# Reordering ScalarE's squares and GpSimd's sums inside the slots of a fused Fourier filter and SwiGLU kernel

## The chip, the cores and the metric

The kernel runs on one core of a Trainium2 chip. A core has five engines that each work through their own queue of instructions in order: TensorE (PE in the profile, its weight loads PEld), VectorE (DVE), ScalarE (ACT), GpSimd (POOL) and SyncE (SP), which here only issues transfers. Sixteen DMA engines move data between the chip's memory and the core, and also transpose tiles inside the core. Matmul results land in eight banks of accumulator memory (PSUM), 512 single-precision numbers wide per partition; an engine must have read a bank before TensorE may write it again.

The metric is the device time of one execution in microseconds (us). Every time below is in us unless it says otherwise.

## What is computed

```python
# x: 8 x 3008 x 256; 1505 frequencies; d_ff = 1536
X = np.fft.rfft(x, axis=1)
Y = X * (filt_r + 1j * filt_i)[None]
y = np.fft.irfft(Y, n=3008, axis=1).reshape(24064, 256)
rms = np.sqrt(np.mean(y * y, axis=-1, keepdims=True) + 1e-06)
yn = y / rms * rms_g
g, v = yn @ w_gate, yn @ w_val
out = (g * (1.0 / (1.0 + np.exp(-g))) * v) @ w_out
```

All inputs and the output are single precision. The kernel multiplies in half precision and accumulates in single precision.

## The kernel before

**The Fourier part** is done for one of the 8 batches `b` at a time, as matmuls with constant tables, because 3008 = 47 x 64:

- *Stage A* (`a_unit`, 12 units a batch): one matmul of 512 columns (`psa`), evicted to `t`; every three units are stored to memory (`z_store`) and loaded back in another layout (`t2_load`).
- *Stage B* (`b_unit`, 16 units): four small matmuls (`psb`, in bank `mb`). VectorE multiplies the result with two parts of the filter (`s_part`, lines 233 and 236), and GpSimd adds the two products into `ss` (`add_unit`, line 270: the "sum"). After two units a transposing transfer on SyncE's queue makes `yt` from `ss` (`yt_load`).
- *The inverse of stage B* (`bi_unit`, 16 units): four small matmuls on `yt` (`psi`, bank `mx`), evicted by ScalarE into `uu` (line 197). All of `uu` is transposed by four transfers (`t4_load`).
- *The inverse of stage A with the norm*, in 6 blocks `m` of up to 512 rows: `n_unit` makes two column blocks of 256 with one matmul (`psn`, bank `mx`) and evicts them to `y`; `sq_unit` squares them on ScalarE, two instructions `junk` (line 324) with a row sum each; `stat_unit` makes the reciprocal root on GpSimd (`u` and `rho`, lines 332 and 334: the "root"); `xt_unit` multiplies `y` with it on GpSimd (`xt`, line 342: the "row scale"); `tr_unit` transposes `xt` into `xn` with a transfer on SyncE's queue.

A few units take other forms: batch 0 and its first blocks go another way before the main loop, and `b_soft` moves both products of four stage B units of batch 1 to GpSimd.

**The feed-forward part** is the main loop. Its items are (batch, block, `jt`) with `jt` from 0 to 11 over the 1536 hidden columns in steps of 128: 576 items. One pass of the loop is a *slot*, numbered like its item; in it `gv` issues two matmuls for the gate (`pg`) and two for the value (`pv`), each over the block's 512 rows (384 in the last block of an even batch), then ScalarE's `sg` and VectorE's `hh`; then come the planned units of that slot; last `down` issues four matmuls (`po`; three for 384 rows) that use the `hh` of two slots before. `pg` and `pv` have two banks each, so four banks serve `gv`; two serve `po`, and `mx` and `mb` the Fourier units. Stage A uses `mx`, or `mb` where that suits better.

**The plan** is a dictionary from a slot to a list of units, filled ahead of the loop: while the loop works on batch `b-1`, the Fourier part of batch `b` is spread over its slots. `fit` looks for a slot in which bank `mx` (`"M"`) or `mb` (`"B"`) is free and the estimated load of ScalarE and VectorE stays within bounds. Units of one slot are issued in list order, and each engine's queue has that order. `at` appends a unit to its slot's list, except those in `front`, which it puts at the head. A batch's second product is planned in the slot after its stage B unit, the sum one slot later, and `yt_load` one slot after every second sum; `sq_unit` stands in the slot after its `n_unit`. `stat_unit`, `xt_unit` and `tr_unit` stand 2, 3 and 7 slots after the second `n_unit` of their block from batch 2 on.

```python
front = (sq_unit, s_part)
...
        if fn in front:
            todo.insert(0, (fn, a))
        else:
            todo.append((fn, a))
...
                    s0 = fit(slots[i], *need)
                    at(s0, b_unit, b, i, 0 if k == "M" else 3)
                    at(s0 + 1, s_part, b, i, 1)
                    at(s0 + 2, add_unit, b, i)
```

Of the kernel before, what the change touches and what calls it, by code (L numbers as in the profile page):

```python
# [100 lines left out]
def kernel(  # L101
# [510 lines left out]
    with tc.manual_schedule():  # L612
# [76 lines left out]

        items = [(b, m, jt) for b in range(B) for m in range(6) for jt in range(JT)]  # L690
        plan, late = {}, {}
        front = (sq_unit, s_part)
        load = {r: [0.0] * (len(items) + 99) for r in "MBAV"}
        room = {"A": 0.8, "V": 0.7}
        for i in range(JT + 1, len(items), JT):
# [29 lines left out]
        def norm_plan(b, m, slots, r):  # L725
            for i in range(2):
                s = fit(slots[i], ("M", 0, 1), ("A", 0, 0.6), ("A", 1, 0.82))
                at(s, n_unit, b, m, i)
                at(s + 1, sq_unit, b, m, i)
            for d, fn in zip(r, (stat_unit, xt_unit, tr_unit)):  # L730
                at(s + d, fn, b, m)
            assert s + r[-1] + 1 < 72 * b + 12 * m
# [49 lines left out]
        for b in range(1, B):  # L782
# [18 lines left out]
            for m in range(6):  # L801
                norm_plan(b, m, (n_at + 8 * m, n_at + 8 * m + (4 if b > 1 else 2)), (2, 3, 7) if b > 1 else (2, 3, 6))

        stores = {}
        for i in range(len(items) + 4):
            if i < len(items):
# [46 lines left out]
```

## Time and profile before

| | us |
|---|---|
| median of 3 runs | 873.1 |
| lowest, highest | 871.36, 873.5 |
| the profiled execution, whole | 872.03 |
| its span, first to last instruction | 870.3 |
| mean granted TensorE clock in it | 0.998 of full |

The page gives for every engine the time that it was busy, its share of the span and the number of its instructions. The chain of work is followed back from the last instruction to what released each step; its shares say whose work set the end. A wait is shown with the engine that waited, its line, and what ended it. In rows in order of time the first number is the start from the beginning of the span, the second the length; then follow engine, line, operation, output and inputs, shape, count, and in brackets an idle time before it with what ended it. A row of the view of stretches gives a stretch's bounds and length, then for each engine the busy time with the number of instructions in it, then the granted clock, the share of the DMA engines and the rate in GB/s. A matmul's end is modelled in these records, its start is not.

### The profile page before, as it was taken

The page shows a single profiled execution, that of the slowest core. Times are in us where ns is not written, and L with a number is a line of the kernel's source. Part 1 is how long each engine was busy: PE and PEld are TensorE (multiplying, and loading weights), DVE is VectorE, ACT ScalarE, POOL GpSimd, SP SyncE. Part 2 cuts the span into 40 slices and gives each one's busy share as a digit, 9 for nine tenths or more (in the row PEclk, how much of TensorE's full clock was granted, in tenths as well). Part 3 has the DMA queues.
Part 4 walks back from the last instruction along what each step waited for, and adds up shares of the span by engine and source line. Part 5 has one row for each costly group of instructions (what it writes and reads, how often), then busy time and mean ns, then how long its engine had stood idle before and what let it go on. Part 6 is the DMA issues. An engine that isn't in the chain of part 4 may idle for free.

```text
span 870.3 us, 17008 instructions
## 1 busy us (share of the span) xinstructions
PE 852.1 (98%) x6129; PEld 533.0 (61%) x6129; DVE 559.9 (64%) x936; ACT 612.1 (70%) x1352; POOL 295.5 (34%) x340
## 2 busy tenths in 40 slices
PE   6999999999999999999999999999999999999997
PEld 5755666566665566666566666666666666665664
DVE  5856765776666666666576666667666766555554
ACT  4787777787577766877578765788567865777443
POOL 4813841454143421444034430443214440132000
PEclk9999999999999999999999999999999999999999
DMA  9986678655976666744656666634474331522101
GB/s 283 270 149 156 119 152 191 147 117 139 188 146 124 126 134 131 146 110 101 143 120 136 125 124 136 148 87 92 122 142 92 72 91 43 109 67 49 62 25 49
DMA packets 198605, 107.98 MB, mean 124 GB/s; under 512 B 158966, under 2 KB 182904, under 8 KB 198520
## 3 DMA queue, kind: packets, MB, share of 16 engines
q1 hardware_dynamic: 189896, 85.52, 44.4%
q0 software_dynamic: 8480, 21.24, 12.2%
q8 instruction: 48, 0.79, 0.4%
q14 instruction: 37, 0.30, 0.1%
q10 hardware_dynamic: 144, 0.13, 0.0%
HBM read 45.78 MB, written 35.65 MB: 94 GB/s over the span
## 4 chain that ended last, share of the span: by engine, by line
PE 93%; DVE 2%; DMA 2%; ACT 2%; issue 1%; POOL 0%; POOLq 0%; ACTq 0%
PE po L565 27%; PE pg L548 27%; PE pv L548 26%; PE psb L243 3%; PE psi L287 2%; PE psn L316 2%; PE psa L208 2%; DMA xc<-in_x_dram 1%; PE psy L419 1%; DVE hh L553 1%; DMA yt<-ss 1%; ACT sg L552 1%; PE psf L390 1%; ACT uu L197 0%; PE pst L369 0%
## 5 line engine op out<-in xcount | busy, mean ns | idle before, releaser
L553 DVE TENSOR_TENSOR hh<-pv,sg 128x512 f16<-128x512 f32 (+2 forms) x578 | 391.5, 678 | 289.1 <-ACT sg L552 221.7
L552 ACT ACTIVATE sg<-pg 128x512 f16<-128x512 f32 (+2 forms) x578 | 337.7, 585 | 220.1 <-PE pg L548 215.6
L548 PE MATMUL pg<-xn,wg 128*128 128x512 f16 (+2 forms) x1156 | 337.9, 374 | 0.1
L548 PE MATMUL pv<-xn,wv 128*128 128x512 f16 (+2 forms) x1156 | 337.8, 374 | 0.0
L565 PE MATMUL po<-wo,hh 128*128 128x256 f16 x2256 | 332.5, 272 | 0.0
L565 PEld LDWEIGHTS <-hh 128*128 128x128 f16 x2256 | 213.5, 98 | 108.0 <-issue 4.6
L548 PEld LDWEIGHTS <-wv 128*128 128x128 f16 x1156 | 113.0, 98 | 130.6
L270 POOL TENSOR_TENSOR ss<-s,s 128x384 f16<-128x384 f16 x112 | 101.8, 910 | 247.9 <-DVE s L236 220.7
L548 PEld LDWEIGHTS <-wg 128*128 128x128 f16 x1156 | 111.5, 98 | 17.2 <-issue 0.6
L342 POOL TENSOR_TENSOR xt<-y,rho 128x1024 f16<-128x1024 f32 (+1 forms) x46 | 85.3, 1854 | 2.9
L324 ACT ACTIVATE junk<-y 128x256 f16<-128x256 f32 x180 | 74.3, 413 | 2.8
L233 DVE TENSOR_TENSOR s<-psb,ff 128x384 f16<-128x384 f32 x124 | 67.8, 547 | 1.0 <-PE psb L243 0.9
L236 DVE TENSOR_TENSOR s<-psb,ff 128x384 f16<-128x384 f32 x124 | 67.8, 547 | 0.0
L197 ACT ACTIVATE uu<-psi 128x384 f16<-128x384 f32 x127 | 62.0, 489 | 1.9 <-PE psi L287 1.2
L197 ACT ACTIVATE y<-psn 128x512 f32<-128x512 f32 (+1 forms) x95 | 55.7, 588 | 4.3
L332 POOL TENSOR_SCALAR u<-ss 128x4 f32<-128x4 f32 (+1 forms) x46 | 8.8, 192 | 133.8 <-ACT junk L324 133.5
L287 PEld LDWEIGHTS <-yt 96*128 96x128 f16 x512 | 35.5, 98 | 27.9 <-DMA yt<-ss 1.2
L334 POOL TENSOR_TENSOR rho<-u,mhalf 128x4 f32<-128x4 f32 (+1 forms) x46 | 46.4, 1010 | 3.8
L197 ACT ACTIVATE t<-psa 128x512 f16<-128x512 f32 x71 | 42.1, 596 | 3.3 <-PE psa L208 1.7
L287 PE MATMUL psi<-wi,yt 96*128 96x96 f16 x512 | 43.1, 206 | 0.9 <-DMA yt<-ss 0.8
L243 PE MATMUL psb<-wb,t 96*128 96x96 f16 x480 | 40.5, 208 | 1.9 <-DVE s L236 1.7
L243 PEld LDWEIGHTS <-t 96*128 96x128 f16 x480 | 28.9, 98 | 14.4 <-DVE s L236 5.2
(96 smaller groups left out, 364.5 us busy)
## 6 DMA issues: line engine op xcount, KB each, us to landing
out_dram<-o SPq DMA_DIRECT2D x40, 512.0 KB, 3.5
xc<-in_x_dram POOLq DMA_DIRECT2D x31, 384.0 KB, 5.8
z_tmp<-t SPq DMA_DIRECT2D x28, 384.0 KB, 2.7
t<-z_tmp SPq DMA_DIRECT2D x28, 384.0 KB, 6.1
out_dram<-o SPq DMA_DIRECT2D x7, 384.0 KB, 2.7
fs<-in_filt_i_dram POOLq DMA_DIRECT2D x3, 512.0 KB, 11.4
fs<-in_filt_r_dram POOLq DMA_DIRECT2D x3, 512.0 KB, 11.1
ws<-in_moe_w_gate_dram POOLq DMA_DIRECT2D x3, 512.0 KB, 10.9
```

Source lines behind the costliest of these rows:

```text
L197: nc.scalar.activation(out=out, in_=in_, func=AXT.Copy, **({} if scale is None else {"scale": scale}))
L233: eng.tensor_tensor(out=o, in0=ps, in1=f1, op=ALU.mult)
L236: eng.tensor_tensor(out=o, in0=ps[:, :, ::-1, :], in1=f2, op=ALU.mult)
L243: nc.tensor.matmul(ps[:, ts(k, KR)], st[b]["t2"][kk // KC][:, kk % KC, ds(dh * P, P)], wb[0:KR, kk, :], start=True, stop=True)
L270: nc.gpsimd.tensor_tensor(out=ss3[g % 3][:, :, dh, 0:KR], in0=s[0], in1=s[1], op=ALU.add)
L287: nc.tensor.matmul(ps[:, k, :], yt[0:KR, k, dh, :], wi[0:KR, 4 * g + k, :], start=True, stop=True)
L324: nc.scalar.activation(out=junk, in_=y[:, i, ts(u, D)], func=AXT.Square, accum_out=ss[:, 2 * i + u:2 * i + u + 1])
L342: nc.gpsimd.tensor_tensor(out=xt[:, 0:n, :], in0=y.rearrange("p a (u d) -> p (a u) d", u=2)[:, 0:n, :], in1=rho[:, 0:n].unsqueeze(2).to_br ...
L548: nc.tensor.matmul(ps[:, 0:w], wt[:, dt_, ts(jt, P)], xn[:, q0:q1, dt_, :], start=(dt_ == 0), stop=(dt_ == 1))
L552: nc.scalar.activation(out=sg[:, c], in_=pg[:, 0:w], func=AXT.Silu)
L553: nc.vector.tensor_tensor(out=hh[:, c], in0=pv[:, 0:w], in1=sg[:, c], op=ALU.mult)
L565: nc.tensor.matmul(po[s4 // 2][:, s4 % 2, :], hh[:, ts(s4, P)], wo[:, jt, :], start=(jt == 0 and s4 % 2 == 0), stop=(jt == JT - 1 and (s4 ...
```

## The change

`add_unit` joins the units that are put at the head of their slot's list. When the plan is complete, the list of a slot is sorted in place, with `sq_unit` behind everything else, if the slot holds a `bi_unit` and the next slot holds a stage A unit in bank `mx` (an `a_unit` whose fourth argument is 0). The sort keeps the order of all other units. No unit changes its slot, its engine or its buffers.

```diff
-        front = (sq_unit, s_part)
+        front = (sq_unit, s_part, add_unit)
...
+        for i, now in plan.items():
+            if any(fn == a_unit and a[3] == 0 for fn, a in plan.get(i + 1, ())) and bi_unit in [fn for fn, _ in now]:
+                now.sort(key=lambda u: u[0] == sq_unit)
+
         stores = {}
```

On the engines' queues this gives: TensorE, VectorE and SyncE have the same instructions in the same order as before. On ScalarE a pair of squares (one square in slot 172) and the eviction `uu` change places in 14 slots. On GpSimd 16 sums stand ahead of a root, a row scale or an input load that they followed before. Two examples, as lists of units:

```text
slot 140, before   s_part(3,5,1)  sq_unit(2,1,1)  bi_unit(3,2)
slot 140, after    s_part(3,5,1)  bi_unit(3,2)  sq_unit(2,1,1)
slot 141, both     ... a_unit(4,3) in bank mx
slot 244, before   xt_unit(3,5)  add_unit(4,13)
slot 244, after    add_unit(4,13)  xt_unit(3,5)
slot 245, both     yt_load(4,6)  ...
```

## The prediction

> **What bounds the kernel now.** I read the page first: busy time per engine, then the chain that ended last.
>
> ```profile
> span 870.3 us, 17008 instructions
> PE 852.1 (98%) x6129; PEld 533.0 (61%) x6129; DVE 559.9 (64%) x936; ACT 612.1 (70%) x1352; POOL 295.5 (34%) x340
> PE 93%; DVE 2%; DMA 2%; ACT 2%; issue 1%; POOL 0%; POOLq 0%; ACTq 0%
> ```
>
> TensorE's own instructions set the end. The change neither adds nor removes an instruction, so it can only give back time in which TensorE stood still. The view of waits, for TensorE alone, names the two waits that it can reach (total, times, longest):
>
> ```profile
> PE psi L287 <- DMA yt<-ss: 0.8, 1, 0.8
> PE psa L208 <- ACT uu L197: 0.5, 2, 0.2
> ```
>
> These rows are too small. A matmul's busy time covers part of a stall, so I measured slots, from the first `pg` matmul of one to that of the next, with the view of stretches (length, then busy time of PE, PEld, DVE, ACT, POOL, clock, DMA):
>
> ```profile
> 250.24:252.00 1.76, 1.67 (x11) 0.87 (x9) 1.12 (x3) 1.73 (x7) 0.74 (x1) 1.00 0.94 232
> 293.35:295.11 1.76, 1.67 (x11) 0.87 (x9) 1.12 (x3) 1.73 (x7) 0.89 (x2) 1.00 0.20 37
> 305.46:306.97 1.51, 1.51 (x11) 0.88 (x9) 1.19 (x3) 1.36 (x5) 1.20 (x3) 1.00 0.00 0
> 347.18:348.78 1.60, 1.60 (x12) 0.87 (x9) 0.95 (x3) 1.59 (x5) 0.91 (x2) 1.00 0.00 0
> 398.24:399.84 1.60, 1.60 (x12) 0.88 (x9) 0.96 (x3) 1.59 (x5) 0.00 (x0) 1.00 0.94 107
> 357.18:358.78 1.60, 1.35 (x11) 0.78 (x9) 0.93 (x3) 1.48 (x6) 0.80 (x2) 1.00 1.62 221
> 362.27:363.87 1.60, 1.35 (x11) 0.78 (x9) 0.93 (x3) 1.48 (x6) 0.35 (x1) 1.00 0.50 35
> 561.56:562.75 1.19, 1.19 (x11) 0.78 (x8) 0.56 (x1) 1.16 (x6) 0.69 (x2) 1.00 1.04 341
> 414.18:416.75 2.57, 1.81 (x19) 1.04 (x17) 1.51 (x3) 1.01 (x2) 0.00 (x0) 1.00 1.16 273
> 345.54:347.18 1.64, 1.64 (x19) 1.12 (x16) 0.82 (x2) 1.35 (x4) 0.00 (x0) 1.00 0.01 5
> ```
>
> The first two are the first and last of six slots with the same matmuls (four of 512 columns, a stage A unit, four of 256); the third has those matmuls and no wait: 1.51. The next two are the first and last of five with the same matmuls at 1.60. Then come the two of 384 columns at 1.60, with their undisturbed twin at 1.19; then the slot of item 250 at 2.57, whose twin (inverse plus stage B) takes 1.64. The clock is 1.00 in all, so no clock explains them.
>
> **Squares behind the eviction.** The edit swaps two neighbours on ScalarE in 14 slots (136, 140, 148, 152, 160, 164, 172, 202, 210, 214, 222, 226, 234, 238), those before a stage A unit in bank `mx`. The slots just measured are the ones that follow thirteen of them; after slot 172, whose unit squares one column block only, I find no stall. Here is slots 136 and 137 in order of time:
>
> ```profile
> 249.39 0.60 ACT L552 ACTIVATE sg<-pg 128x512 f16<-128x512 f32 x1 [0.88 <-PE pg L548]
> 249.63 0.34 PE L287 MATMUL psi<-wi,yt 96*128 96x96 f16 x4
> 249.89 0.41 ACT L324 ACTIVATE junk<-y 128x256 f16<-128x256 f32 x1
> 250.24 0.59 PE L548 MATMUL pg<-xn,wg 128*128 128x512 f16 x2
> 250.83 0.47 ACT L197 ACTIVATE uu<-psi 128x384 f16<-128x384 f32 x1
> 251.20 0.59 ACT L552 ACTIVATE sg<-pg 128x512 f16<-128x512 f32 x1
> 251.35 0.38 PE L208 MATMUL psa<-xc,wa 128*128 128x512 f16 x1
> 251.57 0.60 PE L565 MATMUL po<-wo,hh 128*128 128x256 f16 x4
> 251.82 0.69 DVE L553 TENSOR_TENSOR hh<-pv,sg 128x512 f16<-128x512 f32 x1 [0.64 <-ACT sg L552]
> 252.00 0.59 PE L548 MATMUL pg<-xn,wg 128*128 128x512 f16 x2
> ```
>
> `psi` is complete at 249.97, `uu` leaves its bank only at 250.83+0.47 = 251.30, and `psa`, which goes into that bank, starts at 251.35. Without a wait it would start at 251.35-0.25 = 251.10. The squares hold ScalarE 250.83-249.89 = 0.94 ahead of `uu`. After the swap `uu` follows `sg`; its added wait is for `psi`: 249.97 and 0.05 (as from 251.30 to 251.35), so it runs from 250.02 to 250.49, 0.6 before `psa` wants the bank. The squares then run from 250.39 (`uu` holds the queue 251.20-250.83 = 0.37) to 251.33, and the next `sg` starts there instead of 251.20: 0.13 late. Behind it queue the eviction of `psa` and VectorE's `hh`, at 251.95 instead of 251.82. The down matmuls that read this `hh` come two slots later. Four gate and value matmuls take 0.86 (250.24 to 251.10), four down matmuls 0.43 (251.57 to 252.00), so they start at 252.00+0.86+0.43+0.86 = 254.15 or later, and `hh` ends at 252.64; the cover is 1.5. So I price the lateness at nothing, and if the cover were gone at 14 x 0.13 = 1.8.
>
> In slots 202 to 238 a stage B unit stands between, but on TensorE and VectorE only; ScalarE's order is the same. The gain per slot is bounded by the difference to the twin (above) and by nothing (below): 6 x 0.25 = 1.50, 5 x 0.09 = 0.45, 2 x 0.41 = 0.82, together 2.77. I take the upper end, since the bank is free 0.6 ahead. It stays taken if ScalarE keeps up over longer stretches, two periods of four slots:
>
> ```profile
> 248.76:254.99 6.23, 6.14 (x44) 3.66 (x42) 3.31 (x6) 4.54 (x11) 1.83 (x3) 1.00 1.09 252
> 355.86:360.95 5.09, 4.84 (x41) 3.27 (x39) 3.16 (x7) 4.33 (x12) 3.00 (x4) 1.00 1.05 192
> ```
>
> ScalarE works 4.54 of what becomes 5.98, and 4.33 of what becomes 4.68: tight in the second, but not full. The squares' sums reach GpSimd some 0.5 later; its `xt` has more room than that (below).
>
> **Sums ahead of the scale.** On GpSimd 16 sums move: two pass an `xt` in slots 25 and 88 (the latter an input load too), slot 79 passes the root and an input load, slot 95 the root, six in slots 133 to 173 the root, and six in slots 204 to 244 an `xt`. Nothing moves on SyncE's queue. The one that pays is slot 244 (rows of the chain of waits; after the dots, of the order of time and of the view of tile `yt`):
>
> ```profile
> 406.62 0.25 POOL xt L342
> 406.87 1.60 issue
> 408.47 0.92 POOL ss L270
> 409.41 6.50 DMA yt<-ss
> 415.96 0.34 PE psi L287 x4
> ...
> 406.26 0.55 DVE L236 TENSOR_TENSOR s<-psb,ff 128x384 f16<-128x384 f32 x1
> 409.32 0.64 POOL L188 DMA_DIRECT2D xc<-in_x_dram  x1
> 412.76 2.20 SPq L351 DMA_TRANSPOSE xn<-xt  x1
> DMA to landing us min/median/max: 3.0/3.3/6.5
> ```
>
> The sum's inputs are ready at 406.81, but it stands behind `xt` until 408.47, and the transpose goes out at 409.41, beside a 384 KB input load, and takes 6.50, the longest of all. Put first, the sum runs from about 406.9 to 407.8 and the transpose starts at 407.85. Even at 6.50 it lands at 414.35; `psi` wanted it at 415.96-0.93 = 415.03. So the whole 2.57-1.64 = 0.93 goes; lower bound nothing, if it landed later than the slowest row. What is later: `xt`, by 407.8-406.62 = 1.2, and the input load behind it; its transpose left at 412.76, 4.3 after `xt` made way for the sum at 408.47, so it has room.
>
> For the other fifteen I find no slot whose TensorE wait they end; they are priced at nothing. The added wait: a sum now holds GpSimd's queue until VectorE's product is there, and behind it stand root, scale and, in slots 79 and 88, an input load that stage A uses 18 slots later; the scale's transpose waits in turn, with all that SyncE has behind it. Slot 204 shows the cover:
>
> ```profile
> 349.18 1.89 POOL L342 TENSOR_TENSOR xt<-y,rho 128x1024 f16<-128x1024 f32 x1
> 354.72 2.06 SPq L351 DMA_TRANSPOSE xn<-xt  x1
> ```
>
> `xt` ends at 351.07 and its transpose leaves at 354.72: 3.65 of room. The product follows `hh`, which ends some 0.6 into the slot (252.64-252.00), so it is there at 348.78+0.6+0.55 = 349.9, the sum ends at 350.85, and `xt` is 1.7 late. Without cover the block that needs it would start 1.7 later.
>
> **Sum.** 2.77 + 0.93 = 3.70 off the profiled execution's 872.03 (span 870.3, 1.7 around it): 868.3. The median, 873.1, lies 1.1 above that execution, so 869.4 us is the prediction for the median, 0.42% less.
>
> **The rivals.**
> *The wait only moves* (0.12). In the disturbed slots ScalarE is busy 1.73 of 1.76 and 1.59 of 1.60; order does not shorten its work, so `sg` would become the late one and TensorE would wait for it a slot or two later. For it: those rows. Against: 4.54 of 6.23 over the period. Then only 0.93 is left: 873.1-0.9 = 872.2.
> *A smaller gain* (0.13): one part is not had. Without the tight 384-column pair it is 3.70-0.82, 870.2; if the long landing moves to another transpose that is needed as soon, 3.70-0.93, 870.3. For it: the load at 409.32 met the transpose at 409.41. The Trainium skill (DMA: Bandwidth & Descriptors, section Issuing engines are not separate DMA queues) says that transfers share the same engines and interleave whoever issues them; by it a transpose that leaves 1.56 earlier meets others instead.
> *Only the listed waits are real* (0.06): 0.5+0.8 = 1.3, 871.8; the lengths of the twins speak against it. The Trainium skill (Perfetto Trace Analysis, section Tensor Engine Instruction (MATMUL, LD_WEIGHTS)) says that a matmul's end in the profile is computed from its size, not observed. The rows agree: PE reads 1.60 busy of 1.60 in a slot 0.09 longer than its twin. By the Trainium skill the listed waits are then no upper bound, and the sum by twins stands.
> *ScalarE held behind the inverse* (0.07), slower. `uu` now stands ahead of squares and `sg`, so a late transpose stalls ScalarE too. It decides once `psi` ends later than the `sg` ahead of it by more than the cover of 1.5. The wait at 415.96 (0.93) is the nearest row; at all 14 slots it would cost 13.0, less 3.7: 882.4; it is slower by 0.3% from 0.45 a slot on. Against it: in the rows above `psi` ends 0.02 before `sg`.
> *The order has no effect* (0.05): 873.1.
>
> **Chances and range.** The forecast has 0.57. A difference of 0.3% (2.6 us) is about what can be told from no change. The three runs lie 2.1 apart, so a median can be off by about 1: the forecast covers 868.2 to 870.6. Adding the smaller gains and the moved wait reaches 872.4; down to 867.6 for the runs' scatter. Faster, below 870.5: nine tenths and more of 0.57 (0.53), most of 0.13 (0.09), and 0.03 by scatter from the next two, 0.65. Same: what is left of these and no effect, 0.28. Slower: 0.07.
>
> **What would show it.** Right: slots after the 14 swaps of 1.51 (1.19 with 384 columns), item 250's of 1.64, `psa` waiting for `uu` no more, `uu` 0.1 or less after `psi`, `yt` of slot 245 issued 1.5 earlier, `sg` 0.13 later. Wrong: 1.60 or more left in those slots, a new wait of `pg` on `sg` or of `po` on `hh`, or `xn` late at a block's first matmul.

## The result and the profile after

| | before | changed |
|---|---|---|
| median, us (runs) | 872.55 (7) | 869.75 (7) |
| lowest, highest | 871.14, 873.5 | 868.98, 870.33 |
| profiled execution, whole | 872.03 | 869.23 |
| first slot of the main loop starts at | 47.77 | 48.37 |
| last pair of `pg` matmuls of the main loop starts at | 863.10 | 860.21 |
| main loop between the two | 815.33 | 811.84 |

The ratio changed to before is 0.997, with a 95% interval of 0.9959 to 0.9982: faster by about 0.3%, 2.8 us. The last slot is issued in two halves, and its second half starts with that last pair. The main loop between the two points became 3.48 shorter (815.33 less 811.84, before rounding); the first slot started 0.60 later in this execution, although nothing ahead of it differs between the kernels. That part is taken up again below. Two lines of the changed kernel's page answer to those of before: busy time by engine, chain of work by engine.

```profile
PE 851.3 (98%) x6129; PEld 533.8 (62%) x6129; DVE 559.8 (65%) x936; ACT 612.3 (71%) x1352; POOL 295.9 (34%) x340
PE 96%; DVE 1%; DMA 1%; ACT 1%; issue 0%; SPq 0%
```

TensorE's share of the chain rose from 93% to 96%: less of the chain is somebody else's. TensorE's busy time fell by only 0.8. Between the two points of the table it fell by 1.73 (813.05 to 811.32) of the 3.48: about half of what went had been recorded as busy time, so neither busy nor idle time gives the size of a stall. So I compared the two kernels slot by slot, each from its first `pg` to the next slot's first `pg`. All slots agree within 0.025, but for fifteen. Here are the view of stretches of the changed kernel for the first of the six slots, the first of the five, the first of the two with 384 columns, item 250, and a slot that was not on the list, item 204 (length, then busy PE, PEld, DVE, ACT, POOL, clock, DMA):

```profile
250.81:252.33 1.52, 1.52 (x11) 0.88 (x9) 0.95 (x2) 1.49 (x6) 0.49 (x1) 1.00 0.85 216
346.24:347.75 1.51, 1.51 (x11) 0.88 (x9) 0.77 (x2) 1.48 (x6) 0.07 (x1) 1.00 0.01 5
356.36:357.55 1.19, 1.19 (x11) 0.78 (x8) 0.74 (x2) 1.16 (x6) 0.00 (x0) 1.00 2.55 160
412.21:413.86 1.65, 1.65 (x19) 1.12 (x17) 1.04 (x2) 1.01 (x2) 0.00 (x0) 1.00 1.11 106
347.75:349.26 1.51, 1.47 (x12) 0.87 (x10) 1.16 (x3) 1.43 (x4) 1.16 (x2) 1.00 0.00 0
```

Six slots went from 1.77 to 1.52 (together 1.51), five from 1.60 to 1.52 (0.41), two from 1.60 to 1.19 (0.81), item 250 from 2.57 to 1.65 (0.92): 3.66 gained, added before rounding. Item 204 is a loss; the same stretch of the kernel before is

```profile
348.78:350.08 1.30, 1.30 (x11) 0.88 (x9) 1.23 (x3) 1.08 (x3) 1.22 (x2) 1.00 0.00 0
```

so 0.20 went back there: 3.46 of the loop's 3.48.

How a slot gained is seen in the order of time of the changed kernel, slots 136 and 137:

```profile
250.20 0.34 PE L287 MATMUL psi<-wi,yt 96*128 96x96 f16 x4
250.58 0.49 ACT L197 ACTIVATE uu<-psi 128x384 f16<-128x384 f32 x1
250.81 0.59 PE L548 MATMUL pg<-xn,wg 128*128 128x512 f16 x2
250.96 0.41 ACT L324 ACTIVATE junk<-y 128x256 f16<-128x256 f32 x1
251.68 0.38 PE L208 MATMUL psa<-xc,wa 128*128 128x512 f16 x1
251.91 0.58 ACT L552 ACTIVATE sg<-pg 128x512 f16<-128x512 f32 x1
```

`psi` is complete at 250.54 and `uu` starts at 250.58. It leaves the bank at 251.07; `psa` takes it at 251.68, 0.87 after the slot's start, when its own turn comes. The second `sg` starts 1.10 after the slot's start (251.91-250.81), where it was 0.96 (251.20-250.24): 0.14 late, and no slot behind it is longer.

Item 250 in the order of time, from the transpose's side, followed by the landing row of tile `yt`:

```profile
404.30 0.55 DVE L236 TENSOR_TENSOR s<-psb,ff 128x384 f16<-128x384 f32 x1
404.93 0.91 POOL L270 TENSOR_TENSOR ss<-s,s 128x384 f16<-128x384 f16 x1 [0.35 <-DVE s L236]
405.86 1.26 SPq L277 DMA_TRANSPOSE yt<-ss  x1
407.63 0.64 POOL L188 DMA_DIRECT2D xc<-in_x_dram  x1
```

```profile
DMA to landing us min/median/max: 3.1/3.1/3.1
```

The sum follows its product by 0.08; the transpose leaves 1.77 ahead of the input load instead of 0.09 behind it, and takes 3.1 instead of 6.50.

The loss at item 204 starts two slots earlier, in slot 202, in the changed kernel's order of time:

```profile
345.46 0.34 PE L287 MATMUL psi<-wi,yt 96*128 96x96 f16 x4
346.16 0.49 ACT L197 ACTIVATE uu<-psi 128x384 f16<-128x384 f32 x1 [0.33 <-PE psb L243]
347.49 0.58 ACT L552 ACTIVATE sg<-pg 128x512 f16<-128x512 f32 x1
347.97 0.59 ACT L197 ACTIVATE t<-psa 128x512 f16<-128x512 f32 x1
348.61 0.38 PE L208 MATMUL psa<-xc,wa 128*128 128x512 f16 x1
```

`psi` ends at 345.80, but `uu` starts at 346.16: 0.36 behind it, where the other evictions follow by 0.04. The view of this line's instructions on ScalarE's own sequencer has, in the same stretch,

```profile
L197 ACTq EVENT_SEMAPHORE  x3: 17/38/469, 345.2 to 345.4; - x3
```

three semaphore instructions ahead of this `uu`. It is the first inverse of its batch, and the instruction waits for six semaphores in the program: four of transfers, one each of TensorE and GpSimd. By the trace, the condition of `psi` was the last to be met, and the third semaphore instruction ends right behind it, at 345.83; `uu` starts some 0.32 after that. The bracket names `psb`, the matmuls behind `psi`, which `uu` does not read; in slot 210 the same matmuls follow and `uu` starts 0.04 behind `psi`. So none of the six explains the late start. Everything behind this `uu` on ScalarE moves: squares, `sg`, then `t`, which frees the bank for the `psa` of item 204 at 348.56; that `psa` starts at 348.61.

### The profile page after: what moved, and what is told of

Same layout as the page of the kernel before. It is cut to its first block, busy times and chain, and to the rows that moved or that the text cites. A ratio compares the mean times of both kernels' runs of the same rounds, so it can differ in the third digit from the quotient of the medians.

```text
span 867.4 us, 17011 instructions
## 1 busy us (share of the span) xinstructions
PE 851.3 (98%) x6129; PEld 533.8 (62%) x6129; DVE 559.8 (65%) x936; ACT 612.3 (71%) x1352; POOL 295.9 (34%) x340
## 4 chain that ended last, share of the span: by engine, by line
PE 96%; DVE 1%; DMA 1%; ACT 1%; issue 0%; SPq 0%
PE po L565 28%; PE pg L548 28%; PE pv L548 28%; PE psb L243 3%; PE psi L287 3%; PE psn L316 2%; PE psa L208 2%; PE psy L419 1%; PE psf L390 1%; DMA tail<-in_moe_rms_g_dram 1%; PE pst L369 0%; PE psa L359 0%; PE pf L427 0%; DVE hh L553 0%; DVE s L236 0%
```

## The experiments

The kernel before gave a median of 872.1 (21 runs) beside the first four experiments, and 871.57 (8 runs) beside the last four. "Loop" below is the time between the two points of the table above, in the run's profile. Each edit is shown against the changed kernel, unless its heading says the kernel before.

**The squares alone.**

```diff
-        front = (sq_unit, s_part, add_unit)
+        front = (sq_unit, s_part)
```

> The squares move, the sums stay where they were. Theory (the two parts act in different slots and add up): the thirteen slots behind a swap take 1.52 (1.19 with 384 columns) as in the changed kernel, the slot of item 204 takes 1.50 instead of 1.30, the slot of item 250 keeps its 2.57. From the first slot to the last that is 2.74 - 0.20 = 2.54 less than before, a median of about 870.0. Rival (the sums' earlier transposes are what frees the inverse early enough for the swap): some of the thirteen slots keep 1.60 or more, and less than 2.0 is gained.

Measured: 870.33 (869.44 to 871.52, 11 runs), ratio 0.998 (0.9971 to 0.9989). The loop is shorter by 1.77 only. All thirteen slots behave as in the changed kernel, item 204 costs its 0.20, item 250 keeps its stall, and a slot that had none gets one: item 219, 1.91 before, is now 2.76. View of stretches (items 210 and 219), then four pieces of the chain of work, of this kernel:

```profile
354.10:355.42 1.32, 1.32 (x17) 1.02 (x15) 0.69 (x2) 1.26 (x3) 0.11 (x1) 1.00 1.05 270
365.15:367.91 2.76, 2.08 (x21) 1.26 (x18) 2.06 (x4) 2.29 (x7) 1.23 (x2) 1.00 1.18 317
```

```profile
356.64 0.19 POOL u L332
359.86 0.92 POOL ss L270
360.80 6.01 DMA yt<-ss
366.85 0.34 PE psi L287 x4
```

The chain runs from `uu` through the squares behind it, the root, the scale and the sum into a transpose that takes 6.01, and `psi` waits for it. The kernel before had the same transpose beside the same input load, in its order of time:

```profile
357.89 0.19 POOL L332 TENSOR_SCALAR u<-ss 128x4 f32<-128x4 f32 x1 [1.93 <-ACT junk L324]
361.97 0.65 POOL L188 DMA_DIRECT2D xc<-in_x_dram  x1
362.05 1.26 SPq L277 DMA_TRANSPOSE yt<-ss  x1
368.58 0.34 PE L287 MATMUL psi<-wi,yt 96*128 96x96 f16 x4
```

There `psi` came 6.53 after the issue, in its own time. Two things used up that room. The root starts 2.54 after the start of item 210 (356.64-354.10) instead of 2.03 (357.89-355.86): the squares, now behind `uu`, reach GpSimd 0.51 later, and root, scale, sum and transpose follow. And TensorE, freed of 2 x 0.41 at items 211 and 215, wants `psi` 0.81 earlier. Together 1.32, so `psi` wants the transpose 5.2 after its issue, and 6.05 is 0.85 too much. With the sums moved as well, this sum stands ahead of the scale, and the transpose leaves before the load.

**The sums alone.**

```diff
-        for i, now in plan.items():
-            if any(fn == a_unit and a[3] == 0 for fn, a in plan.get(i + 1, ())) and bi_unit in [fn for fn, _ in now]:
-                now.sort(key=lambda u: u[0] == sq_unit)
```

> The sums move, the squares stay. Theory: only the slot of item 250 changes, 2.57 to 1.64, so 0.93 from the first slot to the last, a median of about 871.6; the thirteen slots keep 1.77 and 1.60, item 204 keeps 1.30. Rival (the sums also pay elsewhere, or cost somewhere by holding GpSimd for a product): other slots change by more than 0.05.

Measured: 870.9 (870.36 to 872.48, 11 runs), ratio 0.9991 (0.9982 to 0.9999); loop shorter by 0.92. One slot of all changed, item 250. View of stretches, item 250:

```profile
413.91:415.55 1.64, 1.64 (x18) 1.12 (x16) 1.03 (x2) 1.00 (x2) 0.00 (x0) 1.00 1.10 104
```

The other fifteen moved sums change nothing that TensorE sees. The parts do not add up: 1.77 + 0.92 = 2.69, together they give 3.48. On top of the squares the sums are worth 1.71 of loop, since they also take away the stall at item 219.

**The swap everywhere but at a batch's first inverse.**

```diff
-            if any(...) and bi_unit in [fn for fn, _ in now]:
+            if any(...) and any(fn == bi_unit and a[1] for fn, a in now):
```

> The changed kernel without the swap in slot 202, where the inverse is the first of its batch. Theory (its eviction waits for six semaphores, most of them in instructions of ScalarE's own queue ahead of it, and that handling, 0.33, delays the next sg and so the bank that item 204 wants): item 204 back at 1.30, item 203 back at 1.60, all other slots as in the changed kernel; 0.12 less from the first slot to the last than the changed kernel. Rival (item 204 is late because two stage A units in a row need ScalarE behind squares, whatever the eviction waits for): item 204 stays near 1.50 or another slot takes the 0.2 over.

Measured: 868.03 in one run; loop 811.74. View of stretches, items 203 and 204:

```profile
345.20:346.80 1.60, 1.60 (x12) 0.88 (x10) 0.95 (x3) 1.59 (x5) 0.91 (x2) 1.00 0.00 0
346.80:348.10 1.30, 1.30 (x12) 0.88 (x9) 1.23 (x3) 1.08 (x3) 0.57 (x2) 1.00 0.00 0
```

Item 204 is back at 1.30 and item 203 at 1.60: the swap of slot 202 gained 0.08 and cost 0.20. The run takes this swap away as a whole, so alone it does not tell what item 204 paid for, the late `uu` or only the squares behind it; the squares computed twice, below, tell. What was expected, that handling six semaphores costs the 0.33, is not borne out. In the changed kernel's own trace the first inverses of batches 1, 5, 6 and 7 have three semaphore instructions and six conditions as well, and their `uu` starts 0.09 behind `psi` (0.086 to 0.087 before rounding). That of batch 6, in order of time:

```profile
550.49 0.34 PE L287 MATMUL psi<-wi,yt 96*128 96x96 f16 x4
550.91 0.49 ACT L197 ACTIVATE uu<-psi 128x384 f16<-128x384 f32 x1
```

**The kernel before, with the input load of slot 247 three slots later.**

```diff
-                        at(max(s + 2, XAT.get(b + 1, (0,) * 4)[i // 3]), x_load, b + 1, i // 3)
+                        at(max(s + 2, XAT.get(b + 1, (0,) * 4)[i // 3]) + 3 * (b == 5 and i == 11), x_load, b + 1, i // 3)
```

> The kernel before, with the input load of slot 247 issued in slot 250 instead, nothing else moved. Theory A (item 250 waited because the transpose met that load): the transpose still leaves at about 409.4, but lands after 3.0 to 3.5 instead of 6.5, and item 250 takes 1.64. Theory B (it waited because the sum, and so the transpose, came late): the landing stays above 6, and item 250 keeps about 2.57.

Measured: 871.97 in one run, whose first slot started at 48.62; loop shorter by 0.93. Its order of time, item 250 in the view of stretches, and the landing row of tile `yt`:

```profile
410.25 2.01 SPq L277 DMA_TRANSPOSE yt<-ss  x1
414.47 0.64 POOL L188 DMA_DIRECT2D xc<-in_x_dram  x1
```

```profile
415.02:416.67 1.65, 1.65 (x19) 1.12 (x16) 1.04 (x2) 1.01 (x2) 0.09 (x1) 1.00 1.06 134
```

```profile
DMA to landing us min/median/max: 3.3/3.3/3.3
```

The sum stands behind the scale here and the transpose leaves as late as before (410.25-0.85 of later start = 409.40, then 409.41). Without the load beside it, it lands after 3.3 and the whole stall is gone. So the meeting, not the late issue, made item 250 long.

**The swap in more slots.** It is made also where the next slot holds an inverse of stage B (`bi_unit`) or of stage A (`n_unit`), not only stage A in `mx`; the first inverses are left as they were.

```diff
+            if any(fn in (n_unit, bi_unit) or fn == a_unit and a[3] == 0 for fn, a in plan.get(i + 1, ())) and any(fn == bi_unit and a[1] for fn, a in now):
```

> The changed kernel with two edits of the condition: the next slot may hold any unit that takes bank mx (an inverse or a norm unit too), and the first inverse of a batch is left out. Theory (the squares delay whatever takes that bank next): item 35 goes from 1.90 to 1.65, item 93 from 1.94 to 1.69, item 101 from 1.60 to 1.52, items 44 and 45 lose 0.1 each, item 204 is back at 1.30, item 203 at 1.60; in all 0.8 to 0.9 less from the first slot to the last than the changed kernel, a median about 0.9 under it. Rival (there ScalarE or VectorE is the late one, not the order): items 35 and 93 keep their length or the next slots grow by as much.

Measured: 868.61 (867.87 to 869.47, 5 runs), ratio to before 0.9962 (0.9948 to 0.9976); loop 4.07 shorter than before and 0.59 shorter than the changed kernel. The stretches of items 35 and 45, the changed kernel's first, then this kernel's:

```profile
101.57:103.47 1.90, 1.81 (x19) 1.12 (x16) 0.79 (x2) 1.87 (x8) 1.45 (x3) 1.00 0.30 64
117.69:119.49 1.80, 1.80 (x15) 1.08 (x13) 1.62 (x3) 1.33 (x5) 1.23 (x2) 1.00 0.04 9
```

```profile
101.62:103.26 1.64, 1.64 (x18) 1.12 (x16) 0.48 (x1) 1.61 (x7) 0.80 (x3) 1.00 0.23 49
117.41:119.41 2.00, 1.86 (x16) 1.08 (x13) 1.87 (x4) 1.73 (x6) 1.29 (x2) 1.00 0.03 8
```

Item 35 gains 0.25 before rounding, and item 93 as much in the same view, but item 45 gives 0.20 back. Its `psa` goes into bank `mb`, in this kernel's order of time:

```profile
118.14 0.55 DVE L236 TENSOR_TENSOR s<-psb,ff 128x384 f16<-128x384 f32 x1
118.75 0.39 PE L208 MATMUL psa<-xc,wa 128*128 128x512 f16 x1
```

VectorE's product frees that bank at 118.69, and `psa` starts 0.06 later. TensorE came there earlier, VectorE hardly did: the wait moved from bank `mx` to bank `mb`. The loop was expected to be 0.8 to 0.9 shorter than the changed kernel's; item 45, which was to lose 0.1 and gained 0.20, makes the difference.

**The changed kernel once more,** with more runs.

> The changed kernel once more, beside the others on one chip. Theory (the loop is the same from run to run, and the start scatters): every slot from item 130 on as in its first profile, the loop 3.5 shorter than before, and a first slot that starts between 47.3 and 48.6; a median 0.8 to 0.9 over that of the widened condition. Rival (the gain depends on chip and run): slots that differ by more than 0.05.

Measured: 869.0 (868.0 to 869.61, 5 runs), ratio 0.9966 (0.9953 to 0.9979). Loop 811.85; every slot as in its first profile. The first slot started at 48.80, a little later than the 47.3 to 48.6 that were expected. Against the swap in more slots (868.61) the medians don't tell the two apart.

**The changed kernel, with the squares of the fourteen slots computed twice.** The second result overwrites the first with the same value.

```diff
                 now.sort(key=lambda u: u[0] == sq_unit)
+                now += [u for u in now if u[0] == sq_unit]
```

> The changed kernel with the squares of the 14 swapped slots computed twice, 0.94 more on ScalarE behind the eviction in each (the same sums are written again). Theory (ScalarE has a cover of 1.5 behind a swap, and room over a period of four slots with 512 columns, but only 0.35 with 384): the slots 137 to 165 keep 1.52, and the stretch with 384 columns (items 204 to 215) grows by 1 to 2.5. Rival (ScalarE is the bound in these slots, order or not): items 137 to 165 grow by some 0.9 each as well.

Measured: 873.81 in one run; loop 4.23 longer than the changed kernel's. View of stretches, items 137, 139 and 204:

```profile
251.23:252.74 1.51, 1.51 (x11) 0.88 (x9) 0.94 (x2) 1.48 (x7) 0.49 (x1) 1.00 0.86 207
254.04:255.87 1.83, 1.83 (x16) 1.04 (x13) 1.55 (x3) 1.67 (x4) 0.00 (x0) 1.00 1.15 131
348.99:351.15 2.16, 1.46 (x11) 0.87 (x9) 1.15 (x3) 2.08 (x6) 1.23 (x2) 1.00 0.00 0
```

The six slots of 512 columns take the doubled squares (0.94 more of ScalarE each) without growing; two slots on, six items from 139 to 167 grow by 0.14 each. The order of time around item 139 shows what was late:

```profile
253.87 0.69 DVE L553 TENSOR_TENSOR hh<-pv,sg 128x512 f16<-128x512 f32 x1 [1.70 <-ACT sg L552]
254.61 0.59 PE L548 MATMUL pv<-xn,wv 128*128 128x512 f16 x2
```

`hh` reads its `pv` bank until 254.56, and the `pv` of item 139 takes that bank at 254.61. So of the 0.94 by which `sg` was later, 0.94-0.14 = 0.80 was covered. Where the slots have 384 columns and less room, items 204, 212 and 213 and item 216 just behind them grew by 2.2 together. Items 228 and 240 grew by 0.60 each, which none of the expectations had: there two stage A units follow each other.

The run also settles item 204. Its slot 202 in order of time:

```profile
346.69 0.34 PE L287 MATMUL psi<-wi,yt 96*128 96x96 f16 x4
347.12 0.49 ACT L197 ACTIVATE uu<-psi 128x384 f16<-128x384 f32 x1
```

This is the same instruction with the same conditions, and it starts 0.09 behind `psi` instead of 0.36, so 0.28 sooner. Item 204 grew by 0.66 (2.164 less 1.505, before rounding), which is the 0.94 of added squares less this 0.28. So the late start passes to item 204 in full, and since 0.28 is more than the 0.20 that the changed kernel lost there, by this sum the swap without it would have cost item 204 nothing.

**The squares alone, with the loads of slots 213 and 247 three slots later.**

```diff
-        front = (sq_unit, s_part, add_unit)
+        front = (sq_unit, s_part)
...
+                        at(max(s + 2, XAT.get(b + 1, (0,) * 4)[i // 3]) + 3 * (b == 5 and i in (2, 11)), x_load, b + 1, i // 3)
```

> Squares only, as in the run with the squares alone, but the two input loads of slots 213 and 247 issued three slots later. Theory (what the sums' move gave was a transpose ahead of such a load instead of beside it; keeping the load away does the same): item 219 back from 2.76 to 1.91 and item 250 from 2.53 to 1.64, the loop 3.5 shorter than before, as in the changed kernel. Rival (the sum's lateness itself costs): item 219 or 250 keeps a wait of more than 0.3.

Measured: 869.16 in one run; loop 811.86, the changed kernel's 811.84 within 0.02. View of stretches, items 219 and 250:

```profile
366.07:367.98 1.91, 1.91 (x21) 1.34 (x18) 1.21 (x3) 1.88 (x7) 0.39 (x2) 1.00 0.77 127
412.20:413.84 1.64, 1.64 (x18) 1.12 (x16) 1.03 (x2) 1.00 (x2) 0.08 (x1) 1.00 0.93 166
```

Both stalls are gone with no sum moved. All that the second part of the change does for the time is to keep two transposes apart from two input loads.

## Why the prediction was right, point by point

**The squares, 2.77.** Measured 2.74 in the thirteen slots, each at its twin's length, and `psa` waiting for `uu` has left the list of waits. The list had shown 0.5 for it. The Trainium skill (Perfetto Trace Analysis, section Tensor Engine Instruction (MATMUL, LD_WEIGHTS)) says that a matmul's end is computed from its size, and the runs agree: of the 2.74 by which the starts of matmuls moved, 1.70 had been recorded as busy time. With that the rival by which only the listed waits are real falls.

**The sums, 0.93.** The size was right (0.92). The working let the transpose leave early enough to land in time even at 6.50, and the later load shows that it need not have left any earlier. The prediction had the cause among its numbers, the load 0.09 ahead of the transpose, but used it for a rival only. The Trainium skill (DMA: Bandwidth & Descriptors, section Issuing engines are not separate DMA queues) says that transfers interleave whoever issued them; 6.5 beside the load and 3.3 without it agree with that.

**The step that failed: the added wait of `uu`.** The prediction said that it is for `psi`, 0.05. That holds in thirteen of the fourteen slots (0.04). In slot 202 `uu` started 0.36 behind `psi`, and that cost 0.20 at item 204, which the sum did not have. One `uu` was read in the trace and the rest were taken to be like it. Why this one is late stays open. It is not that it is a batch's first inverse, nor its six conditions: four others in the same trace start 0.09 behind `psi`, and so does this one with the squares computed twice. One thing in the traces goes with it. Numbered in order of start, this `uu` is record 832 of ScalarE. Record 1088, 256 later, is a semaphore instruction of batch 5's first inverse, and it starts 0.32 after the one ahead of it (446.10 to 446.42) where the others of its kind start 0.04 after theirs; it does so in the profiles of all kernels but the one with the squares computed twice, whose added instructions shift these numbers, and there neither start is late. So the lateness seems to go with the place in ScalarE's queue. No run was made to test that.

**The room behind the squares.** "The squares' sums reach GpSimd some 0.5 later" was measured as 0.51, but "its `xt` has more room than that" left out the sum queued behind `xt`: with the squares alone, this and the shorter slots cost 0.85 at item 219. In the whole change the moved sum covered it, by luck: nothing in the prediction had asked for that. So the sum of independent terms was right for both parts together and would have been wrong for the first alone by nearly a third of its 2.77: the rival by which the long landing moves to another transpose describes the squares alone, not the change.

**The cover of 1.5 for a late `sg`** was mis-sized: it is 0.80, since the bank of `pv` is wanted before `po` reads `hh`. At a lateness of 0.14 this did not matter, and no slot shows it.

**The wait only moves.** The doubled squares speak against a full ScalarE in the slots of 512 columns: they took 0.94 more each and grew by 0.14. The mechanism does exist: in the version with more swaps a part of the gain reappeared as a wait for bank `mb`.

**ScalarE held behind the inverse** fell: in the fourteen slots the largest start of `uu` behind `psi` is 0.36, once.

**The median.** The forecast took off 3.70, and the medians show 2.8 and, in the repeat, 2.57. That 869.4 still came within 0.35 of the measured 869.75 is in part luck: it was counted from a median of three runs, 873.1, and seven runs gave 872.55. Of what the gain fell short, 0.20 is item 204. In the profiled pair the rest lies ahead of the loop: 3.48 of loop less 0.60 of later start is 2.88 of the 2.80 seen. The first slot starts between 47.31 and 48.80 in the ten profiles of this study, in kernels that are the same up to there. Whether the kernel before starts earlier as a rule, or did so by chance in its one profile, is open.

## What to carry to other kernels

Measure a stall by the distance between starts of equal pieces of work, and size each edit by a twin without the stall; the list of waits can understate it (here 0.5 for 2.74). Before adding up gains, take every transfer that is hidden by little and ask how much sooner its reader comes and how much later it leaves: a gain made upstream can expose it. A transpose that is needed soon should not be issued beside a large load, and moving the load is as good as moving the transpose.

## What the hardware showed

A transpose of the products' sum landed after 5.9 to 6.5 us when it was issued within 0.1 us of a 384 KB input load. The one that feeds item 250 took 6.5 beside the load, 3.1 when it was issued 1.8 ahead of it, and 3.3 and 3.9 when the load was put some 4 behind it. An eviction with three semaphore instructions ahead of it started 0.09 us after the matmul that it followed, against 0.04 for those with none; one of them, at one place of ScalarE's queue, started 0.36 after it, for a cause that stays open. And the same start of a kernel took from 47.3 to 48.8 us to reach the first slot, a scatter of 1.5 us, half of what the whole change brought.
